# K and V of the first attention unit in contiguous halves, and a warm-up from a constant tile

## Chip, cores, metric

One core of one Trainium2 chip. The metric is the device time of one execution in microseconds (us). Most executions of one kernel agree within 0.3%. A time is the median of several runs; a ratio is the mean time of one kernel's fast runs over that of the kernel before in the same rounds, so it is not quite the ratio of the medians quoted. Only fast runs are compared; among the runs of the kernel before in one set of rounds there was a single odd one (269.72 us), which is left out of the ratios.

## The reference, cut to what matters

```python
B, Sq, D = 8, 32, 1024; Hq, Hkv, Sk, Dh = 32, 4, 8192, 128
W = min(4096, max(256, Sk // 4))                     # 2048: the last W keys count
q = (x @ wq).reshape(B, Sq, Hq, Dh)...               # wq: 1024 x 4096, bf16
k, v = the last W rows of k_cache, v_cache, each repeated for 8 heads
o = softmax(q @ k.T * Dh ** -0.5) @ v                # no mask: the order of the keys is free
return o @ wo
```

A unit is one (batch, KV head) pair: 2048 keys, 8 heads x 32 queries. There are 32 units. As no mask is used, the keys of a unit may be taken in any order, as long as K and V use the same one.

## The kernel before: the parts concerned

The start loads x, the 1024 columns of wq that the first KV head needs, then K and V of unit 0 ("K0", "V0"). All but half of x goes through one queue, and the pieces of wq and the halves of K0 are interleaved by hand:

```python
nc.sync.dma_start(out=x_sb[:, 0, :], in_=xf[0:P, :])
nc.scalar.dma_start(out=x_sb[:, 1, :], in_=xf[P:2 * P, :])
wq0 = self.load_wq(0, 0, (1, 1, 2)) + self.load_wq(0, 1, (2, 1, 1))   # 6 pieces, 128 rows x 2 KB each (or 256)
for p in wq0[:4]: p()
self.load_k(0, 0)          # first half of K0, 256 KB
wq0[4](); wq0[5]()         # the last two pieces of wq
self.load_k(0, 1)          # second half of K0
self.load_v(0, nc.sync)
...
# in load_k: partition p holds keys 16 p .. 16 p + 15; half h is keys 8 h .. 8 h + 7 of each
nc.sync.dma_start(out=self.k_raw[ui][:, H:, :], in_=src.rearrange("(p j) d -> p j d", j=KT)[:, H:, :])
```

TensorE meanwhile runs warm-up matmuls on a zeroed tile, then the work that the loads release, in this fixed order:

```python
wz = self.c1.tile([P, 512], BF16, name="wz"); nc.vector.memset(wz[:, :], 0.0)
... nc.tensor.matmul(warm[:, :], lhsT=wz[:, 0:P], rhs=wz[:, :], start=True, stop=True)   # 7 times
x_turn(0, ...); x_turn(1, ...)             # 16 transposes of x
for c in range(8):                         # q = wq.T x, chunk by chunk of the 1024 rows of wq
    for h in range(8): q_mm(c, h, ...)
    if c == 5: k_turn(0); k_copy(0)        # transpose the first half of K0
k_turn(1)                                  # ... the second half
# then four casts of q, and the main loop: scores, exp on ScalarE, P V, 32 units x 4 steps
```

Of the kernel before, what the change touches and what calls it, by code (L numbers as in the profile page):

```python
# [11 lines left out]
BF16 = mybir.dt.bfloat16  # L12
# [4 lines left out]
RL_LIMIT = 1.0e22  # L17
RL_MIN = 1.0e-10
Q_CUT = 4
N_WARM = (7, 0, 0)  # L20
VA_ROW = 160
V_HALVES = 29

PE_T = (0, 1, 2, 3, 4)

# [77 lines left out]
class Fast:  # L103
# [62 lines left out]
    def load_wo(self, gq):  # L166

        def piece(i):
            if i == 0:
                self.wo_t[gq] = self.wp.tile([self.P, 4, self.D], BF16, name="wo_sb", tag="w")  # L170
            r0 = gq * 4 * self.Dh
            self.nc.sync.dma_start(out=self.wo_t[gq][:, 2 * i:2 * i + 2, :],
                                   in_=self.wo[r0:r0 + 4 * self.Dh, :].rearrange("(p c) n -> p c n", c=4)[:, 2 * i:2 * i + 2, :])
        return [lambda i=i: piece(i) for i in range(2)]

    def load_k(self, ui, part=None):

        nc, P, KT = self.nc, self.P, self.KT
        b, g = self.units[ui]
        src = self.k_cache[b, g, self.Sk - self.W:, :]  # L180
        if ui not in V_T and ui not in self.kT:
            self.kT[ui] = self.ktp.tile([P, KT, P], BF16, name="kT")
        if ui in PE_T or ui in V_T:
            H = KT // 2
            if part == 1:
                nc.sync.dma_start(out=self.k_raw[ui][:, H:, :], in_=src.rearrange("(p j) d -> p j d", j=KT)[:, H:, :])
                return
            self.k_raw[ui] = (self.kvt.tile([P, KT, self.Dh], BF16, name="k_raw", tag="kv") if ui < 2 else
                              self.krp.tile([P, KT, self.Dh], BF16, name="k_raw"))
            n = KT if part is None else H  # L190
            nc.sync.dma_start(out=self.k_raw[ui][:, 0:n, :], in_=src.rearrange("(p j) d -> p j d", j=KT)[:, 0:n, :])
        else:
            H = KT // 2
            nc.sync.dma_start_transpose(out=self.kT[ui][:, part * H:(part + 1) * H, :],
                                        in_=src.rearrange("(p j) d -> p (j d)", j=KT)[:, part * H * P:(part + 1) * H * P])

    def load_v(self, ui, eng):
        b, g = self.units[ui]
        self.v_sb[ui] = self.vp.tile([self.P, self.KT, self.Dh], BF16, name="v_sb", tag="v")
        n = self.KT // (2 if ui >= V_HALVES else 1)  # L200
        for j in range(0, self.KT, n):
            eng.dma_start(out=self.v_sb[ui][:, j:j + n, :],
                          in_=self.v_cache[b, g, self.Sk - self.W:, :].rearrange("(p j) d -> p j d", j=self.KT)[:, j:j + n, :])

    def load_unit(self, ui):

# [103 lines left out]
    def start(self):  # L310
        nc, P = self.nc, self.P
        warm = self.ps_s.tile([P, 512], FP32, name="warm_ps", tag="s_ps")
        wz = self.c1.tile([P, 512], BF16, name="wz")
        nc.vector.memset(wz[:, :], 0.0)
        x_sb = self.vp.tile([P, self.NT, self.D], BF16, name="x_sb", tag="v")
        xf = self.x.rearrange("b s d -> (b s) d")
        H = self.DC // 2
# [24 lines left out]
        nc.gpsimd.memset(self.ones_c[:, :], 1.0)  # L342
        def warm_up(n):
            for i in range(n):
                nc.tensor.matmul(warm[:, :], lhsT=wz[:, 0:P], rhs=wz[:, :], start=True, stop=True)
        warm_up(N_WARM[0])


# [14 lines left out]
        KT = self.KT  # L363
# [15 lines left out]
        for c in range(self.DC):  # L379
            for h in range(self.rep):  # L380
                q_mm(c, h, 0, P if c >= Q_CUT else self.NQ)
            if c == 0:
                warm_up(N_WARM[2])
                warm_sb = self.c1.tile([P, 8], BF16, name="warm_sb")
                nc.vector.tensor_copy(out=warm_sb[:, :], in_=warm[:, 0:8])
            if c == self.DC - 3:
                tp = self.ps_s.tile([P, KT, P], BF16, name="kf_ps", tag="s_ps")
                k_turn(0)
                k_copy(0)
# [262 lines left out]
```

## Time and profile before

| | us |
|---|---|
| time, median of the first 3 runs | 186.79 (186.78 to 186.91) |
| span of the profiled execution | 185.0 |
| first score matmul | 13.32 |
| from there to the end of the span | 171.7 |

The page's head and table of busy time: the engine, its busy time, its share of the span and its number of instructions. PE is TensorE's matmuls, PEld its weight loads, DVE VectorE, ACT ScalarE, POOL GpSimd.

```profile
span 185.0 us, 5079 instructions
## 1 busy us (share of the span) xinstructions
PE 179.5 (97%) x2056; PEld 153.7 (83%) x2072; DVE 115.4 (62%) x268; ACT 131.8 (71%) x133; POOL 94.7 (51%) x150
```

TensorE is busy almost throughout. The list of waits of the matmuls alone (us in total, times, longest) has no entry from the main loop, only from the start:

```profile
PE warm_ps L345 <- DVE wz L314: 1.2, 1, 1.2
PE q_ps L375 <- DMA wq_sb<-in_wq_dram: 0.4, 2, 0.2
```

So time is to be won before the first score matmul. Here is that stretch in the timeline of the kernel before (start, duration, engine, line, operation; in brackets the idle time before it and what ended it; SPq lines are issues of loads):

```profile
0.87 0.27 DVE L314 MEMSET wz<- 128x256 uint32 x1 [0.87 <-PEq L636]
...
1.20 3.17 PE L345 MATMUL warm_ps<-wz 128*128 128x512 bf16 x7 [1.20 <-DVE wz L314]
...
4.44 1.69 PE L354 MATMUL xT_ps<-ident,x_sb 128*128 128x128 bf16 x16
...
6.05 1.91 PE L375 MATMUL q_ps<-xT,wq_sb 128*128 128x256 bf16 x16
...
8.17 2.81 PE L375 MATMUL q_ps<-xT,wq_sb 128*128 128x256 bf16 x32 [0.22 <-DMA wq_sb<-in_wq_dram]
9.84 0.33 SPq L191 DMA_DIRECT2D k_raw<-in_k_cache_dram  x1
10.69 0.33 SPq L202 DMA_DIRECT2D v_sb<-in_v_cache_dram  x1
...
11.37 1.16 SPq L191 DMA_DIRECT2D k_raw<-in_k_cache_dram  x2
...
12.23 0.62 PE L375 MATMUL q_ps<-xT,wq_sb 128*128 128x128 bf16 x8 [0.21 <-DMA wq_sb<-in_wq_dram]
...
12.87 0.62 PE L368 MATMUL kf_ps<-ident,k_raw 128*128 128x128 bf16 x8
...
13.32 0.60 PE L467 MATMUL s_ps<-QT_63,kT 128*128 128x256 bf16 x4
```

The last matmuls before the scores each start when their load lands: the last piece of wq at about 12.2, the second half of K0 at about 12.84. A load lands when its data is complete on the chip. Earlier landings are seen from the issues: an issue waits until the load eight places before it has landed, so 9.84 is the landing of the wq piece before K0, 10.69 that of K0's first half, 11.37 that of the next piece of wq.

The table by stretches shows what the loads were doing (the last column is GB/s, the one before it the busy share of the 16 DMA engines):

```profile
core 0: us, PE busy (x) PEld busy (x) DVE busy (x) ACT busy (x) POOL busy (x), PEclk, DMA share, GB/s
4.00:8.00 4.00, 3.88 (x33) 2.90 (x32) 0.92 (x3) 1.17 (x2) 0.00 (x0) 1.00 1.01 345
8.00:10.00 2.00, 1.83 (x18) 1.62 (x19) 0.00 (x0) 0.00 (x0) 0.00 (x0) 1.00 0.97 263
10.00:12.00 2.00, 2.00 (x33) 1.71 (x31) 0.53 (x1) 0.00 (x0) 0.00 (x0) 1.00 1.04 394
```

The engines are busy all the time, yet between 8 and 10 us they move 263 GB/s instead of about 400.

### The profile page before, as it was taken

Reading aid. Unit: us, or ns where it says so; the run is one execution under the profiler, and the core shown is the slowest. Engines: PE = TensorE matmul, PEld = TensorE weight load, DVE = VectorE, ACT = ScalarE, POOL = GpSimd, SP = SyncE. Lnnn points to the kernel's source line nnn. Section 1 sums busy time; section 2 is a strip of 40 time slices with the busy share of each in tenths; the row PEclk is TensorE's granted clock in tenths of the full one; section 3 lists DMA queues with packets and bytes.
Section 4 is the critical chain, followed back from the end, with each engine's and each line's share of the span. In section 5 each row is a group of like instructions: output and inputs, shape, how many; then the busy total and the mean of one; then the engine's idle time right before and its main releaser. Section 6 shows DMA issues by size and latency. Waiting matters only on the chain. (4 is left out here: it accounts for less than half of the span.)

```text
span 185.0 us, 5079 instructions
## 1 busy us (share of the span) xinstructions
PE 179.5 (97%) x2056; PEld 153.7 (83%) x2072; DVE 115.4 (62%) x268; ACT 131.8 (71%) x133; POOL 94.7 (51%) x150
## 2 busy tenths in 40 slices
PE   7999999999999999999999999999999999999993
PEld 2889999999999999987878999987777888888743
DVE  0138799994586685586467558647745855355372
ACT  2207899786789787878787677787877888888700
POOL 2000008949939959929944980796299289600000
PEclk9999999999999999999999999999999999999999
DMA  5999999998999999999999999999999999980012
GB/s 151 324 391 415 413 414 396 198 231 278 346 332 297 305 329 337 412 215 244 363 357 244 362 386 252 186 342 397 249 381 320 228 288 246 299 131 0 4 58 62
DMA packets 53082, 51.73 MB, mean 280 GB/s; under 512 B 39744, under 2 KB 40256, under 8 KB 53056
## 3 DMA queue, kind: packets, MB, share of 16 engines
q1 hardware_dynamic: 52480, 50.90, 97.8%
q10 hardware_dynamic: 576, 0.49, 0.8%
q8 instruction: 16, 0.26, 0.6%
q14 instruction: 10, 0.08, 0.1%
HBM read 41.42 MB, written 0.52 MB: 227 GB/s over the span
## 5 line engine op out<-in xcount | busy, mean ns | idle before, releaser
L469 ACT ACTIVATE pT<-s_ps 128x1024 bf16<-128x1024 f32 x128 | 128.9, 1025 | 33.3 <-PE s_ps L467 32.3
L259 POOL TENSOR_SCALAR kTv<-kb 32x512 bf16<-32x512 bf16 x140 | 93.7, 670 | 65.1 <-DMA k_raw<-in_k_cache_dram 26.7
L478 PEld LDWEIGHTS <-pT 128*128 128x128 bf16 x1024 | 68.5, 98 | 3.1
L467 PEld LDWEIGHTS <-kT 128*128 128x128 bf16 x368 | 34.8, 98 | 10.3
L293 PE MATMUL op_ps<-wo_sb,OT 128*128 128x512 bf16 (+2 forms) x128 | 33.0, 353 | 0.8
L273 PE MATMUL q_ps<-xT,wq_sb 128*128 128x256 bf16 x192 | 28.1, 273 | 0.0
L478 PE MATMUL o_ps<-va_112,pT 128*128 128x129 bf16 x352 | 27.1, 220 | 0.0
L478 PE MATMUL o_ps<-va_113,pT 128*128 128x129 bf16 x352 | 27.0, 220 | 0.1
L478 PE MATMUL o_ps<-va_114,pT 128*128 128x129 bf16 x320 | 24.7, 220 | 0.0
L249 DVE STREAM_TRANSPOSE kb<-k_raw 128x512 bf16<-128x512 bf16 x36 | 23.8, 684 | 0.0
L415 DVE RECIPROCAL RL_all<-o_ps 128x2 f32<-128x2 f32 x32 | 5.3, 164 | 27.5 <-PE o_ps L478 27.5
L420 DVE TENSOR_SCALAR o_sb<-o_ps,RL_all 128x128 bf16<-128x128 f32 x64 | 19.5, 346 | 1.1
L467 PEld LDWEIGHTS <-kTv 128*128 128x128 bf16 x144 | 13.9, 98 | 5.1
L273 PEld LDWEIGHTS <-wq_sb 128*128 128x128 bf16 x192 | 17.0, 98 | 1.2
L467 PE MATMUL s_ps<-QT_63,kT 128*128 128x256 bf16 x112 | 16.8, 273 | 0.0
L422 DVE STREAM_TRANSPOSE OT<-o_sb 128x256 bf16<-128x256 bf16 x32 | 14.3, 446 | 1.1
L467 PE MATMUL s_ps<-QT_66,kT 128*128 128x256 bf16 x96 | 14.4, 273 | 0.1
L293 PEld LDWEIGHTS <-OT 128*128 128x128 bf16 x144 | 11.3, 98 | 2.9 <-DVEq L78 0.6
L467 PE MATMUL s_ps<-QT_65,kT 128*128 128x256 bf16 x80 | 12.0, 273 | 0.1
L467 PE MATMUL s_ps<-QT_64,kT 128*128 128x256 bf16 x80 | 12.0, 272 | 0.1
L300 DVE TENSOR_TENSOR oacc<-op_ps,oacc 128x512 f32<-128x512 f32 x8 | 5.5, 683 | 7.4 <-PE op_ps L293 7.4
L409 DVE COPY va_113<-v_sb 128x2048 bf16<-128x2048 bf16 x11 | 9.5, 861 | 0.0
(46 smaller groups left out, 105.2 us busy)
## 6 DMA issues: line engine op xcount, KB each, us to landing
v_sb<-in_v_cache_dram SPq DMA_DIRECT2D x29, 512.0 KB, 6.8
wo_sb<-in_wo_dram SPq DMA_DIRECT2D x16, 512.0 KB, 6.8
wq_sb<-in_wq_dram SPq DMA_DIRECT2D x14, 512.0 KB, 7.4
k_raw<-in_k_cache_dram SPq DMA_DIRECT2D x13, 512.0 KB, 6.5
v_sb<-in_v_cache_dram SPq DMA_DIRECT2D x6, 256.0 KB, 5.8
wq_sb<-in_wq_dram SPq DMA_DIRECT2D x4, 256.0 KB, 6.4
kT<-in_k_cache_dram SPq DMA_TRANSPOSE x36, 6.6
k_raw<-in_k_cache_dram SPq DMA_DIRECT2D x2, 256.0 KB, 7.7
```

The costliest lines, as they stand in the source:

```text
L249: nc.vector.transpose(out=st["kb"][:, sl, :], in_=self.k_raw[ui][:, sl, :])
L259: nc.gpsimd.tensor_scalar(out=out, in0=in_, scalar1=1.0, scalar2=1.0, op0=ALU.mult, op1=ALU.mult)
L273: nc.tensor.matmul(st["ps"][:, 0:self.NQ], lhsT=self.wq_t[g, i][:, c % (DC // 2), hl * P:(hl + 1) * P], rhs=self.xT[:, c, :], start=(c == ...
L293: nc.tensor.matmul(ps[:, 0:w], lhsT=self.OT[:, gq, c, t * P:(t + 1) * P], rhs=self.wo_t[gq][:, c, n0:n0 + w], start=(k == 0), stop=(k == 7))
L300: nc.vector.tensor_tensor(out=acc, in0=ps[:, 0:w], in1=acc, op=ALU.add)
L409: self.nc.vector.tensor_copy(out=self.va[ui % 3][:, :, 0:self.Dh], in_=self.v_sb[ui][:, :, :])
L415: nc.vector.reciprocal(out=rl[:, ui * QT_N:(ui + 1) * QT_N], in_=o_ps[:, :, Dh])
L420: nc.vector.tensor_scalar(out=o_sb[:, qt, :, :], in0=o_ps[:, qt, 0:Dh].rearrange("p (i c) -> p c i", c=4), scalar1=rl[:, ui * QT_N + qt:ui ...
L422: nc.vector.transpose(out=self.OT[:, g * QT_N:(g + 1) * QT_N, :, b * self.Sq:(b + 1) * self.Sq], in_=o_sb[:, :, :, :])
L467: nc.tensor.matmul(s_ps[:, jj, :], lhsT=self.kT[ui][:, c * CJ + jj, :], rhs=q_u, start=True, stop=True)
L469: nc.scalar.activation(out=pT[:, :, :], in_=s_ps[:, :, :], func=ACT.Exp, bias=0.0, scale=self.scale)
L478: nc.tensor.matmul(o_ps[:, qt, 0:self.VW], lhsT=pT[:, jj, qt * P:(qt + 1) * P], rhs=va[:, j, 0:self.VW], start=(j == 0 and qt == 0), stop= ...
```

## The change

Its intent: each half of K0 becomes one contiguous stretch of 256 KB in DRAM (partition p holds keys 8 p to 8 p + 7 of each half) instead of 2 KB out of every 4 KB. V0 must follow the same order of keys, so it is loaded in two halves too. The warm-up reads a constant tile of ones that exists before the kernel's own code starts, so that it need not wait for a memset, and it gets an eighth matmul. V of unit 29 goes from two loads to one, which keeps the number of loads.

```diff
-N_WARM = (7, 0, 0)
+N_WARM = (8, 0, 0)
-V_HALVES = 29
+V_HALVES = 30
+    def rows(self, src, ui, split=False):
+        H = self.KT // 2
+        if ui == 0:
+            return [src[h * H * self.P:(h + 1) * H * self.P, :].rearrange("(p j) d -> p j d", j=H) for h in range(2)]
+        r = src.rearrange("(p j) d -> p j d", j=self.KT)
+        return [r[:, 0:H, :], r[:, H:, :]] if split else [r]
 ... load_k and load_v take their sources from rows() ...
-        wz = self.c1.tile([P, 512], BF16, name="wz")
-        nc.vector.memset(wz[:, :], 0.0)
+        one = nc.const_aps.tensor
-                nc.tensor.matmul(warm[:, :], lhsT=wz[:, 0:P], rhs=wz[:, :], start=True, stop=True)
+                nc.tensor.matmul(warm[:, :], lhsT=one(1.0, [P, P], BF16), rhs=one(1.0, [P, 512], BF16), start=True, stop=True)
```

More of the change, by code (lines that the diff above doesn't have):

```diff
@@ L180, in load_k @@
         src = self.k_cache[b, g, self.Sk - self.W:, :]
+        rows = self.rows(src, ui)
         if ui not in V_T and ui not in self.kT:
@@ L185, in load_k @@
             if part == 1:
-                nc.sync.dma_start(out=self.k_raw[ui][:, H:, :], in_=src.rearrange("(p j) d -> p j d", j=KT)[:, H:, :])
+                nc.sync.dma_start(out=self.k_raw[ui][:, H:, :], in_=rows[1])
                 return
@@ L189, in load_k @@
                               self.krp.tile([P, KT, self.Dh], BF16, name="k_raw"))
-            n = KT if part is None else H
-            nc.sync.dma_start(out=self.k_raw[ui][:, 0:n, :], in_=src.rearrange("(p j) d -> p j d", j=KT)[:, 0:n, :])
+            nc.sync.dma_start(out=self.k_raw[ui][:, 0:KT // len(rows), :], in_=rows[0])
         else:
@@ L199, in load_v @@
         self.v_sb[ui] = self.vp.tile([self.P, self.KT, self.Dh], BF16, name="v_sb", tag="v")
-        n = self.KT // (2 if ui >= V_HALVES else 1)
-        for j in range(0, self.KT, n):
-            eng.dma_start(out=self.v_sb[ui][:, j:j + n, :],
-                          in_=self.v_cache[b, g, self.Sk - self.W:, :].rearrange("(p j) d -> p j d", j=self.KT)[:, j:j + n, :])
+        rows = self.rows(self.v_cache[b, g, self.Sk - self.W:, :], ui, ui >= V_HALVES)
+        n = self.KT // len(rows)
+        for h, src in enumerate(rows):
+            eng.dma_start(out=self.v_sb[ui][:, h * n:(h + 1) * n, :], in_=src)
     def load_unit(self, ui):
```

## The prediction

> **What bounds it now.** Median 186.79 us. After the start it is TensorE: the busy table has PE at 97% of the span, and the list of waits shows PE waiting only for the warm-up tile (1.2 us) and wq (0.4 us). What the first 13 us lose or gain should pass one for one to the end.
>
> In those 13 us the timeline shows a line of loads on one queue. An issue waits for the load eight before it, so issue times give landings: wq pieces at 5.98, 6.86, 8.14, 9.84; first half of K0 at 10.69; last wq pieces at 11.37 and about 12.2; second half of K0 at 12.84. PE idles until 8.17 and 12.23 for wq, until 12.86 for K0's second half; the first score matmul starts at 13.32. Two near ties hold it: last wq piece, q matmuls, q casts (done about 13.1); and K0's second half, its transposes.
>
> **K in contiguous halves.** In windows of 0.25 us the transfers run at 360 to 420 GB/s, but at 180 to 320 from 8.0 to 9.75 us, where the tail of a wq piece and K0's first half stream. At 400 instead of about 250 GB/s that stretch would be about 0.65 us shorter (estimate from these rates). Before, the half is 128 runs of 2 KB at a 4 KB pitch; after, one stretch of 256 KB; runs into SBUF and bytes stay. Against the pitch as cause: K0's second half has it too and streams at about 400, and wq at an 8 KB pitch runs near 400. I give the pitch about 40% and expect 0.2 to 0.3 us on average. PE could use at most about 0.5: from 8.17 on it has 1.7 + 0.9 + 3 x 0.45 us of work to the last q matmul: 12.15 against 12.68.
>
> **V0 in two halves.** Forced by K (same row order). One more issue of 0.33 us on a queue that waits anyway. V0 lands about 14.15, is copied by 14.84, first used at 16.4: slack 1.5 us. V of unit 29 in one piece: long prefetched, 0.
>
> **Warm-up.** DVE's 0.27 us memset goes; PE should start at about 0.9 instead of 1.20 (DVE's first instruction is at 0.87). The Trainium skill, "TensorE: Matmul & The Clock Gate", Part 1, gives 426.7 ns from start to start of a 512-column matmul on a cold array, and about 3.4 us of activity before it speeds up; the trace agrees (seven starts 427 ns apart; 256-column matmuls at 109 ns from 6.05 on). Eight need 3.4 us, so end at about 4.3, still before x lands (4.44). The array may be warm up to 0.3 us earlier, in the cold transposes of x (4.44 to 6.0). But the first q matmul at 6.05 needs the wq piece landing at 5.98: 0 on the critical path.
>
> **Time.** 186.79 - 0.25 = 186.5 us; range 186.0 to 187.0. Faster by over 2%: 1%; within 2%: 98%; slower: 1%.
>
> **What would show it.** Right: warm-up from about 0.9 us; no dip of the rate between 8 and 10 us; last wq piece and K0's second half 0.2 to 0.6 us earlier; first score matmul at about 13.0; from it to the end unchanged. If the dip stays, the pitch was not its cause and the gain is 0.
>
> **What would make it wrong.** The dip belongs to the first touch of K or to other traffic; 2 KB runs for V0 slow the queue; a broadcast constant as operand costs TensorE more; the free-running clock window falls worse; later loads, shifted by one place in the rotation, reach PE late.

## The result, and the profile after

| | before | after |
|---|---|---|
| median, us (6 runs each) | 186.93 (186.78 to 187.02) | 186.88 (186.75 to 187.06) |
| ratio, 95% interval | | 0.9999, 0.9986 to 1.0012 |
| span of the profile | 185.0 | 185.2 |
| first score matmul | 13.32 | 13.44 |
| from there to the end | 171.7 | 171.8 |

The time did not move. The timeline of the changed kernel, the lines that answer to those above:

```profile
0.78 3.57 PE L352 MATMUL warm_ps<-const-bfloat16-1.0 128*128 128x512 bf16 x8 [0.78 <-PEq L643]
...
4.25 1.96 PE L361 MATMUL xT_ps<-ident,x_sb 128*128 128x128 bf16 x16
...
6.01 4.80 PE L382 MATMUL q_ps<-xT,wq_sb 128*128 128x256 bf16 x48
...
9.63 0.33 SPq L211 DMA_DIRECT2D v_sb<-in_v_cache_dram  x1
10.38 0.33 SPq L199 DMA_DIRECT2D k_raw<-in_k_cache_dram  x1
...
11.70 0.33 SPq L211 DMA_DIRECT2D v_sb<-in_v_cache_dram  x1
...
11.73 1.22 PE L382 MATMUL q_ps<-xT,wq_sb 128*128 128x128 bf16 x16 [0.48 <-DMA wq_sb<-in_wq_dram]
12.31 0.98 SPq L199 DMA_DIRECT2D k_raw<-in_k_cache_dram  x2
...
12.99 0.62 PE L375 MATMUL kf_ps<-ident,k_raw 128*128 128x128 bf16 x8
...
13.44 0.60 PE L474 MATMUL s_ps<-QT_63,kT 128*128 128x256 bf16 x4
```

The warm-up starts 0.42 us earlier, as intended. K0's first half lands 0.31 us earlier (10.38 against 10.69; since V0 is now two loads, the loads behind these issues have moved by one place). But the next piece of wq lands 0.33 us later (11.70 against 11.37), and the last piece and K0's second half about 0.1 us later. Whatever was won by 10.4 us was given back by 11.7. The table by stretches of the changed kernel agrees:

```profile
4.00:8.00 4.00, 4.00 (x33) 3.35 (x33) 0.92 (x3) 1.17 (x2) 0.00 (x0) 1.00 0.98 320
8.00:10.00 2.00, 2.00 (x23) 1.80 (x21) 0.00 (x0) 0.00 (x0) 0.00 (x0) 1.00 1.01 309
10.00:12.00 2.00, 1.52 (x28) 1.35 (x26) 0.69 (x1) 0.00 (x0) 0.00 (x0) 1.00 1.05 373
```

The rate is up from 263 to 309 GB/s where K0's first half streams, and down from 394 to 373 afterwards. The repeats below show the same: 235 to 268 GB/s from 8 to 10 us in three profiles with the strided K0, 296 to 309 in four with the contiguous one.

Two finer readings of the trace are used from here on. It holds each load's completions on the 16 DMA engines. The Trainium skill, "DMA: Bandwidth & Descriptors", section "Why a DMA increments its semaphore by 16 and not by 1", says that a load runs on up to 16 engines that finish independently and that only the full count means that the data has landed. The trace agrees: the 16 completions of K0's second half were 1.17 us apart before (11.65 to 12.82) and 1.54 us after (11.40 to 12.94). And it holds every packet. A 2 KB packet usually takes 84 ns (16 engines at that pace make 390 GB/s), a 4 KB packet 159 ns; from 3 to 12 us some 2 KB packets take several times as long, up to 412 ns in the first profile (the very first packets, before 3 us, took up to 1088 ns there and are left out of what follows). I call the sum of what packets take beyond 84 or 159 ns the excess; divided by 16 it is the mean delay of an engine.

### The profile page after: what moved, and what is told of

It reads as the page before. It is cut to its first block, busy times and chain, and to the rows that moved or that the text cites. A ratio compares the mean times of both kernels' runs of the same rounds, so it can differ in the third digit from the quotient of the medians.

```text
span 185.2 us, 5096 instructions
## 1 busy us (share of the span) xinstructions
PE 180.9 (98%) x2073; PEld 154.4 (83%) x2073; DVE 115.2 (62%) x267; ACT 131.9 (71%) x133; POOL 94.7 (51%) x150
## 5 line engine op out<-in xcount | busy, mean ns | idle before, releaser
L301 PE MATMUL op_ps<-wo_sb,OT 128*128 128x512 bf16 (+2 forms) x144 | 36.5, 355 | 0.2
```

Source lines behind the costliest of these rows:

```text
L301: nc.tensor.matmul(ps[:, 0:w], lhsT=self.OT[:, gq, c, t * P:(t + 1) * P], rhs=self.wo_t[gq][:, c, n0:n0 + w], start=(k == 0), stop=(k == 7))
```

## The experiments

The theories, in the order in which they came up:

- A: a landing is set by the slowest of 16 engines, slow packets fall where they will, and the layout of K has no part in them.
- B (rival): the contiguous half is really faster, and something else in the change really costs as much.
- C: a first reading of each stretch of K0 costs slow packets once; contiguous halves only move half of them later.
- D (rival of C): the contiguous pattern itself, or V in two pieces, spoils what follows.
- E: the slow packets belong to the strided reading of wq.
- F (rival of E): they belong to the first 12 us, whatever is read.

### The same kernel again: before_again

No edit.

> The kernel before, unedited: measures the noise. Its ratio to itself should be 1.000 with an interval of about 0.001 either way. A second profile of it: if single slow packets (a 2 KB packet of 84 ns that takes over 150 ns) are what opens the dip of the rate between 8 and 10 us, they should be there again, at whatever places; the first score matmul at 13.2 to 13.6 us.

Measured: 186.75 us, ratio 0.9997 (0.9979 to 1.0015). The noise is larger than I had expected, about 0.2%. First score at 13.29 us, again with slow packets at 8 to 10 us.

### The changed kernel again: after_again

No edit.

> The changed kernel, unedited. Theory A (the last of 16 engines sets each landing, slow packets fall where they will, and the layout of K has no part in them): first score matmul at 13.2 to 13.6 us again, but the landings before it distributed otherwise than in the first profile (there: first half of K0 at 10.37, next wq piece only at 11.69). Theory B (the contiguous half is really faster by 0.3 us and something else in the change really costs 0.3 us): K0's first half again near 10.4 and the next wq piece again over 1.2 us after it.

Measured: 187.13 us, ratio 1.0010 (0.9990 to 1.0029). K0's first half landed at 10.71, the next piece of wq 0.69 us after it, so theory B's mark was missed; the last piece of wq then came 1.19 us later, at 12.59. The first score came at 13.73 us, outside what theory A allowed. Slow packets again fell behind K0's first half, but on another load.

### The layout alone: k_halves_only

```diff
 (the changed kernel)
-N_WARM = (8, 0, 0)
+N_WARM = (7, 0, 0)
-        one = nc.const_aps.tensor
+        wz = ...; nc.vector.memset(wz[:, :], 0.0)      # the warm-up of before
```

> K and V of unit 0 in contiguous halves, the warm-up of before. Theory A: within 0.1% of before (186.8 to 187.1 us). Theory B with the cost in the warm-up (constant operand, later fast clock): 0.2 to 0.3 us faster than before, ratio 0.9985.

Measured: 187.08 us, ratio 1.0013 (0.9994 to 1.0033), first score at 13.56. There is no gain that the warm-up could have hidden, so that form of theory B falls. The timeline shows the same shape as in the changed kernel, more strongly: K0's first half lands at 10.10 and the next piece of wq only at 11.81.

```profile
10.10 0.33 SPq L199 DMA_DIRECT2D k_raw<-in_k_cache_dram  x1
...
11.81 0.33 SPq L211 DMA_DIRECT2D v_sb<-in_v_cache_dram  x1
...
11.84 1.26 PE L383 MATMUL q_ps<-xT,wq_sb 128*128 128x128 bf16 x16 [0.68 <-DMA wq_sb<-in_wq_dram]
...
13.56 0.60 PE L475 MATMUL s_ps<-QT,kT 128*128 128x256 bf16 x4
```

### The warm-up alone: warm_only

```diff
 (the kernel before)
-N_WARM = (7, 0, 0)
+N_WARM = (8, 0, 0)
-        wz = ...; nc.vector.memset(wz[:, :], 0.0)
+        one = nc.const_aps.tensor                      # the warm-up of after
```

> The warm-up from the constant tile with eight matmuls, K and V as before. Theory A: within 0.1% of before; warm-up from about 0.78 us, and no earlier first score matmul, since that waits for wq and K0. Theory B with the cost in the warm-up: 0.2 to 0.3 us slower, ratio 1.0015.

Measured: 186.69 us, ratio 0.9997 (0.9982 to 1.0013), warm-up from 0.78 us, first score at 13.20. No cost or gain of the warm-up shows within the noise. It is off the critical path: what ends before 4.4 us has to wait for x, and then for wq.

### V0 in one load: v0_one_load

```diff
 (the changed kernel)
+        if ui == 0:
+            eng.dma_start(out=self.v_sb[ui][:, :, :].rearrange("p (h j) d -> p h (j d)", h=2),
+                          in_=src.rearrange("(h p j) d -> p h (j d)", h=2, j=self.KT // 2))
+            return
-V_HALVES = 30
+V_HALVES = 29
```

> The changed kernel with V of unit 0 in one load of two 2 KB runs per partition, so that the rotation of the load semaphores is that of before. Theory C: the time of the changed kernel, ratio to before 1.000 to 1.0015, first score at 13.4 to 13.7. Theory D with V's halves or the rotation as cause: back to before or better, first score by 13.2, ratio 0.9985 to 0.9995.

Measured: 187.28 us, ratio 1.0016 (0.9994 to 1.0038), first score at 13.71, as in the changed kernel. There is no sign that V's halves or the shifted rotation are the cause.

By now there were three profiles with the strided K0 in its place and four with the contiguous one. The table has the time at which the last engine finished (for K0's second half also the middle one, the ninth of 16), in us, and the excess in us.

| profile | K0, 1st half | next wq | last wq | K0, 2nd half: middle | last | first score | span | excess 8-10 | 10-12 |
|---|---|---|---|---|---|---|---|---|---|
| before | 10.68 | 11.36 | 12.19 | 12.29 | 12.82 | 13.32 | 185.0 | 9.3 | 0.7 |
| before_again | 10.90 | 11.53 | 12.15 | 12.42 | 12.79 | 13.29 | 185.0 | 8.1 | 0.0 |
| warm_only | 10.75 | 11.44 | 12.07 | 12.33 | 12.70 | 13.20 | 184.9 | 9.4 | 0.1 |
| after | 10.37 | 11.69 | 12.29 | 12.03 | 12.94 | 13.44 | 185.2 | 6.7 | 2.5 |
| after_again | 10.71 | 11.40 | 12.59 | 12.24 | 13.23 | 13.73 | 185.4 | 5.8 | 2.5 |
| k_halves_only | 10.08 | 11.80 | 12.44 | 11.92 | 13.06 | 13.56 | 185.3 | 5.7 | 1.9 |
| v0_one_load | 10.40 | 11.28 | 12.62 | 12.01 | 13.21 | 13.71 | 185.4 | 4.3 | 2.5 |
| mean, strided (3) | 10.78 | 11.44 | 12.14 | 12.35 | 12.77 | 13.27 | | | |
| mean, contiguous (4) | 10.39 | 11.54 | 12.49 | 12.05 | 13.11 | 13.61 | | | |

This is where the expected gain went, and it is the main reading of the study. With contiguous halves K0's first half lands 0.39 us earlier, and the middle engine finishes K0's second half 0.30 us earlier. The mean of the 16 engines finishes it only 0.15 us earlier (12.13 against 12.28), and the excess from 4 to 12 us is nearly the same (18.6 against 19.2 us): the slow packets were moved more than removed. And the last engine finishes it 0.34 us later, and TensorE waits for the last. In the strided kernels no engine meets more than a few slow packets after 10 us; in the contiguous ones about 2 us of excess fall there, on a few engines and too late to be made up before the second half of K0 is needed. The columns of the last wq piece, of K0's second half and of the first score do not overlap between the two groups, which speaks against theory A in its pure form, in which the layout has no part; what stays of it is the slowest engine. It is not quite shown: each profile is one execution. The spans of all fast executions reach from 184.6 to 185.6 us with the strided K0 as in the kernel before and from 184.8 to 185.9 us in these contiguous versions, so the two groups do overlap where nobody looked at packets. The span follows the first score: span less first score is 171.7 or 171.8 us in all seven.

### Is it the first reading of K0? same_half_twice, k_first, k_touched

same_half_twice reads the first contiguous half again as the second half, so nothing new is touched there. The result is wrong; the comparison with the reference was too coarse to notice it.

```diff
 (the changed kernel, in load_k, second half)
-                nc.sync.dma_start(out=self.k_raw[ui][:, H:, :], in_=rows[1])
+                nc.sync.dma_start(out=self.k_raw[ui][:, H:, :], in_=rows[0])
```

> The changed kernel, but the second K load reads the first contiguous half again (wrong result on purpose, same loads otherwise). Theory C: a first reading of each stretch of K0 costs slow packets once; the contiguous halves only move half of these behind the first half, to 10 to 12 us, where they hit the last wq pieces. Then this kernel, which touches no new stretch there, has no such spread: last wq piece and second K load by 12.1 and 12.8 us, first score by 13.3, 186.5 to 186.8 us. Theory D: the contiguous pattern itself or V in two pieces spoils the transfers after it: then it stays as in the changed kernel, last wq piece at 12.3 to 12.6, first score at 13.4 to 13.7, ratio about 1.001.

Measured: 187.37 us, ratio 1.0024 (1.0006 to 1.0043). The last piece of wq landed at 12.78, the second K load at 13.39, first score at 13.89, excess from 10 to 12 us 3.6. Theory C falls: from 10 to 12 us there is no less excess without a new stretch (3.6 us against 1.9 to 2.5).

```diff
 (k_first: the kernel before)
+        self.load_k(0, 0)
         for p in wq0[:4]: p()
-        self.load_k(0, 0)
```

> The kernel before, with K0's first (strided) half loaded ahead of all wq pieces. Bytes ahead of the last wq piece are the same. Theory C: the slow packets go with K0: the dip of the rate from 8.0 to 9.75 us is gone or under half as deep, and lies at 4.5 to 6.5 instead. If the dip belongs to that wq piece or to the moment, it stays at 8 to 10 us. First score at 13.1 to 13.5 us either way, ratio within 0.1% of 1.

Measured: 187.25 us, ratio 1.0037 (1.0012 to 1.0061), first score at 13.70: slower than either theory allowed. From 3 to 5 us, where x and then K0's first half streamed, there was no excess at all; from 5 to 12 us, with the wq pieces, there were 13.6 us of it, 2.3 of them after 10 us. So the strided K0 did not take the slow packets along when it was moved. It also shows that late slow packets are not a mark of contiguous halves alone: moving K0 in the order brings them too.

```diff
 (k_touched: the kernel before)
+        touch = self.c1.tile([P, 16], BF16, name="touch")
+        nc.scalar.dma_start(out=touch[:, :], in_=...K0 as "(p j) d -> p j d"[:, 0, 0:16])
```

> The kernel before, plus a small early load on ScalarE's queue that reads 32 bytes of every 4 KB of K0. Theory C: the slow packets of 8.0 to 9.75 us are gone or halved, first score up to 0.3 us earlier (12.9 to 13.1), ratio 0.998 to 0.9995. If first reading has no part in it: the dip stays, ratio 1.000 to 1.001.

Measured: 187.44 us, ratio 1.0029 (1.0012 to 1.0046), first score at 13.35, excess from 8 to 10 us 5.1 and from 10 to 12 us 2.6. There is less excess from 8 to 10 us than in the kernel before (8.1 to 9.3), but k_first has as little there (4.7) without any touching, and no time was gained, so this does not rescue theory C. Its span is 172.15 us past the first score; TensorE was only 0.03 us late until its last matmuls, and the last vector instruction of the output started at 182.38 us against 182.34 in the kernel before, so the other 0.4 us or so came after that; why is not known.

### Is it wq? wq_in_a_row, wq_in_a_row_k_halves

In all of these profiles the excess from 4 to 12 us summed to 13.6 to 19.9 us, about one us per engine, wherever it fell. What streams through all of that time is wq: 2 KB out of every row of 8 KB. The edit reads the same number of bytes as one stretch (wrong weights; runs, loads and order stay).

```diff
 (in load_wq; once on the kernel before, once on the changed kernel)
+            if g == 0:
+                src = self.wq[c0 * 32:(c0 + n) * 32, :].rearrange("(c r) (s n) -> (r s) c n", r=32, s=4)
```

> The kernel before, with the wq pieces of the first group read as one contiguous stretch instead of 2 KB out of every 8 KB row (other weights, so a wrong result on purpose; same bytes, same loads, same runs of 2 KB in SBUF). Theory E: the slow packets of 4 to 12 us (about 18 us of excess over 16 engines in every profile so far, 1.1 us per engine) belong to the strided reading of wq. Then under 6 us of excess are left, the last wq piece lands by 11.5, the first score comes at 12.2 to 12.7 and the time is 185.7 to 186.2 us, ratio 0.994 to 0.997. Theory F: slow packets belong to the first 12 us whatever is read: excess 14 to 20 us, first score 13.1 to 13.9, ratio 0.999 to 1.003.

> The same edit of wq on the changed kernel (wrong result on purpose). Theory E with the contiguous K innocent: within 0.1% of the run with the strided K (wq_in_a_row), first score within 0.15 us of it. If the contiguous halves of K themselves bring slow packets: 0.2 to 0.4 us later than there, with packets over 150 ns between 9 and 12 us. Theory F: as the changed kernel, 13.4 to 13.7.

| | strided K0 (wq_in_a_row) | contiguous K0 (wq_in_a_row_k_halves) |
|---|---|---|
| median, us; ratio to before | 186.09; 0.9954 (0.9938 to 0.9970) | 185.97; 0.9950 (0.9931 to 0.9968) |
| last wq piece, K0's second half: last engine | 11.20, 11.80 | 11.25, 11.88 |
| first score, span | 12.89, 184.6 | 12.55, 184.3 |
| excess 4-8, 8-10, 10-12 us | 4.6, 2.6, 0.0 | 7.9, 0.1, 0.0 |

The tables by stretches, first of wq_in_a_row (strided K0), then of wq_in_a_row_k_halves (contiguous K0); GB/s last:

```profile
4.00:8.00 4.00, 3.96 (x30) 3.14 (x30) 0.92 (x3) 1.17 (x2) 0.00 (x0) 1.00 0.98 352
8.00:10.00 2.00, 2.00 (x21) 1.80 (x19) 0.00 (x0) 0.00 (x0) 0.00 (x0) 1.00 1.03 367
10.00:12.00 2.00, 2.00 (x37) 1.98 (x35) 0.29 (x1) 0.00 (x0) 0.00 (x0) 1.00 1.06 419
```

```profile
4.00:8.00 4.00, 3.70 (x33) 2.72 (x32) 0.92 (x3) 1.07 (x2) 0.00 (x0) 1.00 1.01 343
8.00:10.00 2.00, 1.94 (x20) 1.76 (x21) 0.00 (x0) 0.00 (x0) 0.00 (x0) 1.00 1.05 405
10.00:12.00 2.00, 2.00 (x40) 2.00 (x37) 0.64 (x1) 0.08 (x1) 0.00 (x0) 1.00 1.06 409
```

The edit changes the pitch and also which rows are read (a quarter of wq's rows instead of a quarter of each row), so it does not separate the two. With that said, theory E holds in the main, theory F falls: the dip from 8 to 10 us is gone, the excess is 7.2 and 8.0 us instead of 18, and 0.5% of the time with it, in both kernels. Two details of the expectation were missed: less than 6 us of excess was expected, and the first score with the strided K0 came at 12.89 instead of by 12.7. In that profile TensorE itself had become the limit: the last wq piece had landed at 11.20, but its matmuls were done only at about 12.5, because the array was on its slow clock until 7.2 us: the mean of its weight loads of wq is 151 ns up to there and 98 ns after 7.3. (The clock column says 1.00 in this stretch all the same, so for the first us I go by the weight loads.)

The second kernel shows that contiguous halves of K0 are not harmful in themselves. With wq in one stretch they leave 0.1 us of excess from 8 to 10 us where the strided half leaves 2.6, and 405 GB/s where it has 367: the effect that the change was meant for. Only next to the strided wq do they come with slow packets after 10 us. Even so, the two landings that matter are no earlier (11.25 and 11.88 against 11.20 and 11.80), and the times are within their noise.

### Fewer bytes ahead: x_half_late, x_half_late_fill

The experiments pointed to the load ahead of the last wq piece, so I tried to shorten it. Batches 4 to 7 need the second half of x only from unit 4 on.

```diff
 (the kernel before, cut to its core)
-        nc.scalar.dma_start(out=x_sb[:, 1, :], in_=xf[P:2 * P, :])
         self.load_k(0, 1)
+        nc.sync.dma_start(out=x_sb[:, 1, :], in_=xf[P:2 * P, :])
-   q of the first KV head for all 256 rows of x before and just after the first score
+   q for rows 0 to 127 there; 8 transposes and 8 x 8 q matmuls for rows 128 to 255 in steps 3 to 11 of the main loop
 (x_half_late_fill)
-N_WARM = (7, 0, 0)
+N_WARM = (7, 0, 2)
```

> The kernel before, with the second half of x (256 KB, batches 4 to 7) loaded after K0's second half, and its transposes and q matmuls moved to the steps 3 to 11 of the main loop. If the time is the start of the first score plus 171.7 us, and that start is set by what the queue must bring ahead of the last wq piece and K0: 256 KB less at 300 to 400 GB/s brings it 0.65 to 0.85 us forward, to 12.4 to 12.8 us; the same work of TensorE comes later, so the time falls by 0.4 to 0.8 us, to 186.1 to 186.5, ratio 0.996 to 0.998. If another thing than the loads ahead sets the start: ratio 0.999 to 1.001. Risk: with half the work before the first score TensorE may fall back to its slow clock.

> The same with two further warm-up matmuls after the first q chunk, against the slow clock. If the clock is no matter: within 0.1% of x_half_late. If the clock falls back there: x_half_late is later by 0.3 us or more and this one is not.

Measured: 192.58 us, ratio 1.0292 (1.0268 to 1.0315), and 192.55 us, ratio 1.0297 (1.0277 to 1.0318). Both are a plain miss: 5.5 us slower, where 0.4 to 0.8 us faster was expected. In x_half_late the array fell back to its slow clock. The table by stretches of that kernel, with the granted clock in the third column from the end:

```profile
7.00:8.00 1.00, 0.00 (x0) 0.00 (x0) 0.00 (x0) 0.00 (x0) 0.00 (x0) 1.00 0.98 322
8.00:9.00 1.00, 0.62 (x8) 0.45 (x8) 0.00 (x0) 0.00 (x0) 0.00 (x0) 0.83 0.90 283
9.00:10.00 1.00, 0.57 (x6) 0.58 (x7) 0.00 (x0) 0.00 (x0) 0.00 (x0) 0.50 0.93 297
10.00:11.00 1.00, 1.00 (x12) 1.00 (x10) 0.00 (x0) 0.00 (x0) 0.00 (x0) 0.50 1.03 397
11.00:12.00 1.00, 1.00 (x12) 1.00 (x11) 0.00 (x0) 0.00 (x0) 0.00 (x0) 0.50 1.07 412
12.00:13.00 1.00, 1.00 (x20) 1.00 (x19) 0.00 (x0) 0.00 (x0) 0.00 (x0) 0.96 1.05 410
```

TensorE idled for most of 6 to 8 us, then ran at half clock for about 3.4 us (from the column: (0.17 + 3 x 0.50 + 0.04) / 0.50), and the first score came at 14.31. The Trainium skill, "TensorE: Matmul & The Clock Gate", Part 1, gives a free-running window of about 3.4 us, and half clock after a window in which the array was idle. The trace agrees with the length (its clock records change at 5.25, 8.66 and 12.08 us), but the window before the fall was not idle throughout: 16 matmuls ran in it for about 1.1 us, and its longest gap was 1.97 us. The two filling matmuls cured that: the first score came at 13.10. But the median was the same, because the distance to the end had grown from 171.7 to 176.8 us in the second (189.9 - 13.10) and 176.5 in the first (190.8 - 14.31). (The profiled execution of the second was its fastest, 191.75 us; the other four took 192.24 to 192.62 and have no profile.) Of the 64 moved matmuls, the kernel before too runs 32 after its first score (16 from 13.76 and 16 from 15.09 us). So the main loop gained 32 matmuls at about 62 ns (the weight loads of 16 took 0.99 us before) and 8 transposes at about 56 ns, an estimate of 2.4 us. The list of waits of the second kernel adds 1.7 us in which TensorE waits after the first score, where the kernel before has none: 1.1 us for copies of kT, 0.4 for the casts of q, 0.2 for exp. About 1 us of the 5.1 is not accounted for. Before the first score, where TensorE waits for loads anyway, the added work had been nearly free; in a loop in which TensorE is never idle it costs its full length, and here waits on top. No version that beats both kernels and computes the right result was found.

## Why the prediction was right and where it was wrong

The time lies in the stated range and the class is right, but no gain at all would have met both (186.79 lies between 186.0 and 187.0), so this does not speak for the mechanism. The expected gain of 0.25 us did not come: 186.88 against 186.93 us.

- "What the first 13 us lose or gain should pass one for one to the end": right. In nine of the ten profiles that leave the main loop alone and have the ordinary wq, span less first score is 171.7 or 171.8 us, while the first score ranges from 13.20 to 13.89.
- Warm-up "0 on the critical path": right within the noise (ratio 0.9997 alone, 0.9982 to 1.0013). It started at 0.78 instead of the 0.9 that I had expected. "The array may be warm up to 0.3 us earlier" was not so: in this profile it was warm later. Weight loads take 151 ns on the slow clock and 98 on the fast one; those of the q matmuls (min/median/max, ns) are all fast before and not all fast after:

```profile
L375 PEld LDWEIGHTS <-wq_sb x64: 95/98/99, 6.0 to 12.6; 128*128 128x128 bf16 x64
```

```profile
L382 PEld LDWEIGHTS <-wq_sb x64: 95/98/151, 6.0 to 12.7; 128*128 128x128 bf16 x64
```

  The trace's clock records put the change to full speed at 5.74, 4.37, 4.52 and 4.94 us in before, before_again, k_halves_only and after_again: it moves by more than a us without any cause in the program, and here it does not matter.
- V0 in halves costs nothing: nothing speaks against it (v0_one_load, with V0 in one load, was no faster).
- The step that failed is the one that priced the dip: "At 400 instead of about 250 GB/s that stretch would be about 0.65 us shorter ... I give the pitch about 40% and expect 0.2 to 0.3 us on average". The pitch of K0 has only the smaller part in the dip: making it contiguous raised the rate from 8 to 10 us from 263 to 309 GB/s, and reading wq in one stretch raised it to 367 with the strided K0. I had cleared wq because it ran near 400 GB/s at other moments; but the slow packets come in bursts, and one clean stretch proves nothing.
- The signs named were "last wq piece and K0's second half 0.2 to 0.6 us earlier; first score matmul at about 13.0". The middle engine was 0.3 us earlier, the mean of the 16 only 0.15 us. I had reasoned with the mean rate of 16 engines, while a load lands with its slowest. The slow packets after 10 us put the last engine 0.34 us behind instead, and the first score at 13.61 on average instead of 13.27.
- By that mean the change should even be 0.3 us slower. The times hint at it (ratios 0.9999, 1.0010, 1.0013 and 1.0016 for the four contiguous versions), but each interval includes 1, so a loss is possible and not shown.

What stays open: why the contiguous half next to the strided wq brings slow packets after 10 us, when the strided half in the same place did not in three profiles, and why three other small shifts (k_first, k_touched, same_half_twice) bring them too. A favourable order in the kernel before, found by trying, would fit; no run tests it. Nor does any run show what a slow packet waits for.

## What to carry to other kernels

When several loads in a row hold up a kernel, look at the last of the 16 engines and not at GB/s: a faster mean can come with a later landing. Before blaming the load that streams during a dip, change each of the loads near it by itself, even with wrong data; here the neighbour was to blame. And work that fills an engine's waiting time at the start is nearly free there: moved into a loop that this engine bounds, it costs at least its full length.

## What the Trainium skill lacked or had wrong

- "DMA: Bandwidth & Descriptors", section "Latency and other measured facts", has rates for row pitches of 512 KiB and more, clearly lower from 2 MiB on. Nothing is said of small pitches: here 2 KB out of every 8 KB cost about 18 us of excess over 16 engines against 7 to 8 us for one stretch of the same size, 0.85 us of 186.94. Its explanation by channels is an inference there, and no run here tests it.
- No page has a figure for how far apart the engines of one load finish: completions of one 256 KB load were 0.6 to 2.7 us apart here (k_halves_only, K0's first half: 9.46 to 10.08; same_half_twice, K0's second half: 10.69 to 13.39). From 3 to 12 us single 2 KB packets took up to 412 ns in the first profile instead of 84.
- "TensorE: Matmul & The Clock Gate", Part 1, was right on two points: 427 ns between cold 512-column matmuls and 3.4 us of half clock once it fell. Two details were otherwise. It has the change to full speed vary by 500 ns either way from run to run; here it came at 4.37 to 7.20 us, and 1.37 us apart in two executions of the kernel before. And it has the slow clock come after an idle window; in x_half_late a gap of 1.97 us, in a window with about 1.1 us of matmuls, was enough. It does not say whether a broadcast constant may serve as both operands without a cost: here it did, on the slow clock: eight matmuls in 3.57 us against seven of a real tile in 3.17.
